# LSH attention with a mixture of experts on one core: in pairs 1 to 13 the products with v of two query blocks run together

## Chip, cores and metric

One core of one Trainium2 chip runs the whole program. The metric is the device time of one execution in microseconds (us). Three executions of the kernel before took 709.75, 714.4 and 717.0 us, median 714.4 us. A further execution was profiled.

## The reference, cut to what matters

The first half is attention over 4 batches, 8 heads, 768 tokens, head size 64. Every query and key gets a code of 6 bits (the signs of six projections), and a query sees only the keys with its own code:

```python
mask = q_bucket[:, :, :, None] == k_bucket[:, :, None, :]
scores = scale * np.matmul(q, k.transpose(0, 1, 3, 2))
scores = np.where(mask, scores, -1000000000.0)
attn = np.exp(scores - np.max(scores, axis=-1, keepdims=True))
attn = attn / (np.sum(attn, axis=-1, keepdims=True) + 1e-09)
return np.matmul(attn, v).astype(np.float32)
```

The second half sends each of the 3072 tokens to the one of 8 experts that a gate picks, and computes `gate * (relu(x @ w1) @ w2)` there. The change touches the attention only.

## The kernel before

**Pairs, groups, steps.** Two heads make a pair: 16 pairs, four of them per batch. The 768 queries of a pair fall into two groups of three query blocks (128 queries each). A step is one block of one head, so a group has 6 steps and a pair 12; the loop over `steps` runs 192 times, and `n` is the step's number in its group. Pairs are counted from 0.

**One step.** `scores` (L227) multiplies a query block with all 768 keys, in four TensorE instructions into one of two PSUM buffers `s` (L232, L233; the second operand adds the low parts and the codes). VectorE reads `s` once, writes `p` and the row maximum (L241), which frees the buffer. ScalarE takes the exponential in place (L250). The result must be transposed before it can meet v. In pairs 1 to 13 the steps n = 0, 2, 4 of a group do this through memory: four DMAs write the block out (L260), one brings it back in another order (L263), and VectorE turns 32x32 squares (L266, the "turn") at the first place of the step six later. The steps n = 1, 3, 5 do it on TensorE (`transposes`, L275) with two copies on ScalarE (L278); these stand in steps n = 2, 4 and n = 0 of the next group.

**The products with v.** `av` (L288) makes 12 matrix products for one query block, 24 instructions of L293, into the single PSUM buffer `o`. A group's products are made while the next group's scores run: before the change its blocks 0, 1 and 2 at n = 1, 3 and 5 of the next group. At n = 5 `av_evac` follows, whose copy of `o` (L300) is made by ScalarE in the next step.

**Order.** The order on TensorE, VectorE, ScalarE and SyncE is that of the program; SyncE issues nearly all DMAs, in order. In loop step i TensorE gets, in this order: the scores of step i + 2; a piece of the tail of an earlier group; the codes of the next pair, if due; transposes; products with v. The scores of step i + 2 need the `s` buffer that VectorE's read of step i frees. VectorE gets: the turn, if one is due; the read of step i + 2; the pieces.

**The tails.** At n = 1 `out_and_route` (L744) handles the group before last. In three of four pairs it is `av_out` (L312): three transposes into the single PSUM buffer `misc` (L323), and a VectorE product that reads it (L324). For the last pair of a batch it is the logits (L344), and `av_out`, `gather_heads` (L356), `one_hot`, a pause, `ranks` (L376 to L386; the last VectorE instruction that reads `misc` is L386) and `rows` follow one per step. So the groups with such pieces are both groups of pairs 4, 8, 12 and the first group of pairs 5, 9, 13.

**The codes.** At n = 3 of a pair's first group `pair_codes` (L141) issues 8 TensorE instructions into `misc` (L146) for the next pair; VectorE reads them (L148). In that step no piece of a tail is issued.

The lines that place the products with v, and the tail's piece of a step:

```python
due.append((i + 2, lambda a=prev[0], c=prev[1]: out_and_route(a, c)))
...
side = (g, n) == (0, 3) and 0 < pr < NPR - 1
if due and due[0][0] == i and not last:
    due.pop(0)[1]()
elif light and not side and (not last or n < 2):
    light.pop(0)()
```

Of the kernel before, what the change touches and what calls it, by code (L numbers as in the profile page):

```python
# [58 lines left out]
def lsh_attention_moe_kernel(ctx, tc, qkd, q2d, k2d, v, pjbd, wg, w1, w2, ident_in, tri_in, cols_in, eoff_in, ids_in, out):  # L59
# [228 lines left out]
    def av(pr, g, jj, o):  # L288
        vt = operands[pr][1]
        pt = probs_t(pr, g, jj)  # L290
        for kc in range(NB):
            for hh in range(2):
                PE.matmul(out=o[hh * D:hh * D + D, jj * P:jj * P + P], lhsT=vt[:, kc, hh * D:hh * D + D], rhs=pt[:, hh, kc],  # L293
                          start=kc == 0, stop=kc == NB - 1)

    def av_evac(pr, g, sums, o, defer):
        b, pi = divmod(pr, NPAIR)
        ot = otp.tile([P, 384], F32, name="ot")
        if defer:
            late.append(lambda: A.copy(out=ot, in_=o[:, 0:384]))  # L300
        else:
            V.tensor_copy(out=ot, in_=o[:, 0:384])
        ots[(b, g, pi)] = ot
        if (b, g) not in invs:
            invs[(b, g)] = smp.tile([P, 3, H], F32, name="inv", bufs=4)
        inv = invs[(b, g)][:, :, 2 * pi:2 * pi + 2]
        if defer:
            divide.append(lambda: V.reciprocal(out=inv, in_=sums.rearrange("p (j h) -> p j h", h=2)))
        else:
            V.reciprocal(out=inv, in_=sums.rearrange("p (j h) -> p j h", h=2))  # L310
# [178 lines left out]
    def early_logits(b, g):  # L489

        inv = invs[(b, g)]
        n = NPAIR - 1
        lsb = gp.tile([P, 384], F32, name="lsb", bufs=1)
        lw = gp.tile([P, 3, H, E], F32, name="lw", bufs=1)
        parts.append(gp.tile([P, 3, E], F32, name="part", bufs=1))

        def logits():
            lps = ps_m.tile([P, 512], F32, name="misc")
            for pi in range(n):
                PE.matmul(out=lps[32 * pi:32 * pi + 32, 0:384], lhsT=wg_sb[:, pi, :], rhs=ots[(b, g, pi)], start=True, stop=True)  # L500
            V.tensor_copy(out=lsb[0:32 * n], in_=lps[0:32 * n, 0:384])

        def gather_heads():
            lt = ps_m.tile([P, 512], F32, name="misc")
            for jj in range(3):
                PE.transpose(out=lt[:, jj * P:jj * P + 32 * n], in_=lsb[0:32 * n, jj * P:jj * P + P], identity=ident[0:32 * n, 0:32 * n])
            for jj in range(3):
                V.tensor_tensor(
                    out=lw[:, jj, 0:2 * n].rearrange("p (q h) e -> p q h e", h=2),
                    in0=lt[:, jj * P:jj * P + 32 * n].rearrange("p (q x) -> p q x", x=32)[:, :, 0:2 * E].rearrange("p q (h e) -> p q h e", h=2),  # L510
                    in1=inv[:, jj, 0:2 * n].rearrange("p (q h) -> p q h", h=2).unsqueeze(3).broadcast_to([P, n, 2, E]),
                    op=ALU.mult)

        def total():
            V.reduce_sum(out=parts[0], in_=lw[:, :, 0:2 * n].rearrange("p j h e -> p j e h"), axis=AX.X)

        return [logits, gather_heads, total]

    NPR = B * NPAIR
    MOVES = {(pr, g): (0, 2, 4) for pr in range(1, NPR - 2) for g in range(2)} | {(14, 0): (0, 2), (14, 1): (0,)}  # L520

    def blocks(pr, g):
        if (pr, g) in MOVES:
            return [(1, 0), (0, 0), (2, 0), (1, 1), (2, 1), (0, 1)], (0, 1, 2)
        b = [(jj, hh) for jj in range(3) for hh in range(2)]
        return sorted(b, key=lambda x: x[::-1]) if (pr, g) == (0, 0) else b, (0, 1, 2)
# [217 lines left out]
    def out_and_route(pr, g):  # L744
        while divide:
            divide.pop(0)()
        if pr % NPAIR < NPAIR - 1:
            av_out(pr, g)
            return

        pieces = route(pr // NPAIR, g)
        pieces[0]()
        light.append(lambda: av_out(pr, g))
        light.extend(pieces[1:])
        if (pr, g) == (NPR - NPAIR - 1, 1):
            light.extend(pick_first(light.pop()))
# [16 lines left out]
    for i, (pr, g, jj, hh) in enumerate(steps):  # L773
        n = i % 6
# [46 lines left out]
        last = pr == NPR - 1 and g == 1  # L821
# [13 lines left out]
        if prev is not None:  # L835
            if n == 0:
                o = ps_o.tile([P, 512], F32, name="o")
            order_p = blocks(prev[0], prev[1])[1]
            for jp in (order_p[:2], order_p[2:])[n] if last and n < 2 else order_p[n // 2:n // 2 + 1] if not last and n % 2 == 1 else ():
                av(prev[0], prev[1], jp, o)  # L840
            if n == (1 if last else 5):
                av_evac(prev[0], prev[1], prev[2], o, (prev[0], prev[1]) != (NPR - 2, 1) and not last)
                if not last:
                    due.append((i + 2, lambda a=prev[0], c=prev[1]: out_and_route(a, c)))
                if (prev[0], prev[1]) == (NPR - 2, 1):
                    light += early_logits(B - 1, 1)
# [240 lines left out]
    with tc.manual_schedule(engines={SY.engine}):  # L1087
# [10 lines left out]
        for e in range(E):  # L1098
            last = e + 1 == E
# [154 lines left out]
```

## Time and profile before

| what | value |
|---|---|
| three executions | 709.75, 714.4, 717.0 us (median 714.4) |
| profiled execution | 719.9 us, of which the span 718.1 us and 1.8 us around it |
| mean granted TensorE clock | 0.992 of full speed |
| TensorE, VectorE, ScalarE, GpSimd busy | 97%, 68%, 61%, 57% of the span |
| pairs 1 to 13 in the trace | from 37.5 to 359.8 us |
| a plain second group of a pair | 11.58 us |
| a plain first group of a pair (with codes) | 12.33 us |
| a group with pieces of a batch's tail | 13.35 to 13.62 us |

Busy time of TensorE is a modelled figure, since its instructions overlap; the starts of its instructions show the pace. A group's time is the distance between the starts of its first scores and of the next group's.

### The profile page before, as it was taken

The page shows a single profiled execution, that of the slowest core. Times are in us where ns is not written, and L with a number is a line of the kernel's source. Part 1 is how long each engine was busy: PE and PEld are TensorE (multiplying, and loading weights), DVE is VectorE, ACT ScalarE, POOL GpSimd, SP SyncE. Part 2 cuts the span into 40 slices and gives each one's busy share as a digit, 9 for nine tenths or more (in the row PEclk, how much of TensorE's full clock was granted, in tenths as well). Part 3 has the DMA queues.
Part 4 walks back from the last instruction along what each step waited for, and adds up shares of the span by engine and source line. Part 5 has one row for each costly group of instructions (what it writes and reads, how often), then busy time and mean ns, then how long its engine had stood idle before and what let it go on. Part 6 is the DMA issues. An engine that isn't in the chain of part 4 may idle for free.

```text
span 718.1 us, 16099 instructions
## 1 busy us (share of the span) xinstructions
PE 696.8 (97%) x5735; PEld 615.9 (86%) x5735; DVE 484.8 (68%) x1012; ACT 439.1 (61%) x996; POOL 408.8 (57%) x410
## 2 busy tenths in 40 slices
PE   7999999999999999999999989999999999999996
PEld 3888887788888888888888869999999999988994
DVE  6667878878778877878787656746464656464641
ACT  6887887788887888877777642434343434334330
POOL 3895757686656866676684320056564654707171
PEclk9999999999999999999999999999999999999999
DMA  8989878989988899799886217474746476665421
GB/s 279 294 258 283 276 232 254 290 261 278 281 260 259 250 291 266 235 289 287 230 251 185 89 62 184 118 196 119 196 135 180 145 208 160 207 163 158 147 70 47
DMA packets 110082, 150.34 MB, mean 209 GB/s; under 512 B 12548, under 2 KB 77990, under 8 KB 109992
## 3 DMA queue, kind: packets, MB, share of 16 engines
q1 hardware_dynamic: 105016, 136.52, 65.6%
q0 software_dynamic: 4976, 12.69, 5.0%
q8 instruction: 47, 0.77, 0.4%
q14 instruction: 43, 0.35, 0.1%
HBM read 94.23 MB, written 55.18 MB: 208 GB/s over the span
## 4 chain that ended last, share of the span: by engine, by line
PE 51%; issue 24%; POOL 13%; DMA 6%; DVE 2%; SPq 1%; ACT 1%; POOLq 0%; another core or an unknown queue 0%; DVEq 0%; ACTq 0%
PE o L293 17%; PE s L232 11%; POOL y L1029 11%; PE s L233 9%; PE t L275 9%; PE misc L146 2%; PE misc L323 2%; POOL yo L1027 2%; DMA y<-yo,tok 2%; DMA xr<-xs 1%; DVE p L241 1%; DMA qk<-qkd 1%; PE s L732 1%; DMA wraw<-w 1%; ACT p L250 1%
## 5 line engine op out<-in xcount | busy, mean ns | idle before, releaser
L232 PE MATMUL s<-k,q 128*128 128x512 f32 (+1 forms) x384 | 149.4, 389 | 0.1
L293 PE MATMUL o<-pt,vt 128*64 128x128 f32 x2304 | 146.8, 277 | 0.0
L293 PEld LDWEIGHTS o<-pt,vt 128*64 128x64 f32 x2304 | 123.8, 137 | 23.5 <-issue 18.4
L241 DVE TENSOR_SCALAR_CACHE_REDUCE p<-s 128x768 f32<-128x768 f32 x111 | 106.0, 955 | 35.9 <-PE s L233 31.6
L278 ACT COPY pt<-t 128x384 f32<-128x384 f32 x222 | 95.7, 482 | 52.6 <-PE t L275 46.0
L233 PE MATMUL s<-c 76*128 76x512 f32 (+1 forms) x384 | 124.1, 344 | 0.0
L1029 POOL DMA_INDIRECT y<-yo,tags x88 | 100.4, 1141 | 24.9 <-issue 22.7
L250 ACT ACTIVATE p<-p,m 128x768 f32<-128x768 f32 x111 | 104.4, 941 | 9.4 <-DVE m L244 6.7
L241 DVE TENSOR_SCALAR_CACHE_REDUCE pd<-s 128x768 f32<-128x768 f32 x81 | 76.8, 948 | 33.1 <-PE s L233 11.0
L232 PEld LDWEIGHTS s<-k,q 128*128 128x128 f32 x384 | 73.3, 191 | 27.6 <-issue 14.8
L987 ACT ACTIVATE hh<-hps 128x352 fp32r<-128x352 f32 (+3 forms) x56 | 27.9, 500 | 105.1 <-PE hps L1001 88.0
L275 PE MATMUL t<-ident,p 128*128 128x128 f32 x666 | 92.0, 274 | 0.1
L266 DVE STREAM_TRANSPOSE pt<-pq 128x768 f32<-128x768 f32 x81 | 78.6, 970 | 14.1 <-DMA pq<-moved 11.7
L701 DVE TENSOR_TENSOR wlo<-wraw,whi 128x1024 fp32r<-128x1024 f32 x60 | 72.9, 1217 | 17.4 <-ACT whi L696 15.7
L233 PEld LDWEIGHTS s<-c 76*128 76x128 f32 x384 | 74.0, 193 | 9.2 <-ACT c L208 0.4
L1020 PE MATMUL hps<-hh,whi 128*128 128x448 f32 (+9 forms) x224 | 77.3, 345 | 2.0 <-ACT whi L696 2.0
L275 PEld LDWEIGHTS t<-ident,p 128*128 128x128 f32 x666 | 75.2, 141 | 4.5 <-issue 2.5
L250 ACT ACTIVATE pd<-pd,m 128x768 f32<-128x768 f32 x81 | 75.9, 937 | 5.2 <-DVE m L244 0.8
L1020 PE MATMUL hps<-hh,wlo 128*128 128x436 f32 (+6 forms) x224 | 77.2, 344 | 1.8 <-DVE wlo L701 1.4
L1027 POOL TENSOR_TENSOR yo<-yt,tags 128x512 f32<-128x512 f32 (+3 forms) x25 | 23.2, 950 | 97.3 <-DVE yt L1022 97.2
L1020 PE MATMUL hps<-hl,whi 128*128 128x436 f32 (+6 forms) x224 | 77.1, 344 | 0.0
L1001 PE MATMUL hps<-xh,whi 128*128 128x352 f32 (+3 forms) x224 | 75.2, 336 | 0.0
(226 smaller groups left out, 1284.0 us busy)
## 6 DMA issues: line engine op xcount, KB each, us to landing
wraw<-w SPq DMA_DIRECT2D x64, 512.0 KB
moved<-pd SPq DMA_DIRECT2D x324, 96.0 KB
pq<-moved SPq DMA_DIRECT2D x81, 384.0 KB
qk<-qkd SPq DMA_DIRECT2D x30, 384.0 KB
xs<-zrow SPq DMA_DIRECT2D x8, 910.0 KB
vt<-v SPq DMA_DIRECT2D x16, 384.0 KB
coded<-cr SPq DMA_DIRECT2D x15, 192.0 KB
c<-coded SPq DMA_DIRECT2D x30, 72.0 KB
```

The costliest lines, as they stand in the source:

```text
L232: PE.matmul(out=s[:, c0:c1], lhsT=q1[:, qs], rhs=k1[:, c0:c1], start=True, stop=False)
L233: PE.matmul(out=s[:, c0:c1], lhsT=q2[0:KM, qs], rhs=k2[0:KM, c0:c1], start=False, stop=True)
L241: V.tensor_scalar(out=to, in0=of, scalar1=-0.5 * BIG, scalar2=None, op0=ALU.max, op1=ALU.max, accum_out=m[:, 0:1])
L250: A.activation(p, p, AF.Exp, bias=m[:, 1:2], scale=0.125, accum_out=sums[:, idx:idx + 1])
L266: V.transpose(out=pt()[:, hh].rearrange("p c (s j) -> p c s j", j=SQ), in_=q.rearrange("p s c i -> p c s i"))
L275: PE.transpose(out=t[:, i * P:i * P + P], in_=p[:, kc * P:kc * P + P], identity=ident)
L278: A.copy(out=dst, in_=src)
L293: PE.matmul(out=o[hh * D:hh * D + D, jj * P:jj * P + P], lhsT=vt[:, kc, hh * D:hh * D + D], rhs=pt[:, hh, kc], start=kc == 0, stop=kc == N ...
L701: loeng.tensor_tensor(out=lo[:, i:i + step], in0=cell["t"], in1=bf(hi[:, i:i + step]), op=ALU.subtract)
L1001: PE.matmul(out=hps[:, 0:w], lhsT=wt[:, c, fs], rhs=xt[:, c, 0:w], start=n == 0, stop=n == 3 * NDC - 1)
L1020: PE.matmul(out=yps[:, 0:w], lhsT=wt[:, f, ds], rhs=ht[:, 0:w], start=n == 0, stop=n == 3 * NFC - 1)
L1029: rows_apart("out", G.indirect_dma_start(out=out_seg, out_offset=bass.IndirectOffsetOnAxis(ap=tags[:, i, 0:1].bitcast(I32), axis=0), in_=y ...
```

## The change

In pairs 1 to 13 (`0 < pr < NPR - 2`, with NPR = 16) nothing is multiplied with v at n = 1 any more; the products of the group's first two blocks are issued together at n = 3, where in a pair's first group they stand behind the codes, and those of the third at n = 5 as before. Pairs 0, 14 and 15 keep their order. No instruction is added or removed on any engine, and no buffer changes.

```diff
-            for jp in (order_p[:2], order_p[2:])[n] if last and n < 2 else order_p[n // 2:n // 2 + 1] if not last and n % 2 == 1 else ():
+            if last:
+                now = (order_p[:2], order_p[2:])[n] if n < 2 else ()
+            elif 0 < pr < NPR - 2:
+                now = {3: order_p[:2], 5: order_p[2:]}.get(n, ())
+            else:
+                now = order_p[n // 2:n // 2 + 1] if n % 2 else ()
+            for jp in now:
                 av(prev[0], prev[1], jp, o)
```

## Rows read from the trace of the kernel before

**Rows 1.** Busy time by stretch (PE, PEld, DVE, ACT, POOL; then clock, DMA share), pair 6, first group

```profile
160.40:172.70 12.30, 12.30 (x128) 10.19 (x126) 9.88 (x19) 9.89 (x26) 8.57 (x9) 1.00 0.97 293
```

**Rows 2.** Timeline of TensorE (start, duration, line), a plain second group, from n = 1

```profile
198.78 0.49 PE L323 MATMUL misc<-ident,ot 128*128 128x128 f32 x3
199.21 1.53 PE L293 MATMUL o<-pt,vt 128*64 128x128 f32 x24
200.67 0.50 PE L232 MATMUL s<-k,q 128*128 128x512 f32 x1
201.01 0.40 PE L233 MATMUL s<-c 76*128 76x512 f32 x1
...
201.49 0.82 PE L275 MATMUL t<-ident,p 128*128 128x128 f32 x6
202.06 0.48 PE L232 MATMUL s<-k,q 128*128 128x512 f32 x1
202.38 0.40 PE L233 MATMUL s<-c 76*128 76x512 f32 x1
```

**Rows 3.** Timeline of TensorE, two cuts of the same products with v

```profile
199.37 1.37 PE L293 MATMUL o<-pt,vt 128*64 128x128 f32 x22
...
200.46 0.28 PE L293 MATMUL o<-pt,vt 128*64 128x128 f32 x2
```

**Rows 4.** Timeline of VectorE, pair 6, first group, n = 0

```profile
161.56 0.98 DVE L266 STREAM_TRANSPOSE pt<-pq 128x768 f32<-128x768 f32 x1 [1.51 <-DMA pq<-moved]
162.46 0.92 DVE L241 TENSOR_SCALAR_CACHE_REDUCE pd<-s 128x768 f32<-128x768 f32 x1
```

**Rows 5.** Timeline of TensorE, the same group, n = 1

```profile
162.54 0.49 PE L323 MATMUL misc<-ident,ot 128*128 128x128 f32 x3
```

**Rows 6.** Timeline of VectorE, pair 11, first group, n = 0

```profile
285.83 0.98 DVE L266 STREAM_TRANSPOSE pt<-pq 128x768 f32<-128x768 f32 x1 [2.24 <-DMA pq<-moved]
```

**Rows 7.** Waits of VectorE by line: total us, times, longest

```profile
DVE pt L266 <- DMA pq<-moved: 11.7, 15, 2.2
```

**Rows 8.** Timeline of VectorE, pair 8, first group, n = 2

```profile
211.96 0.98 DVE L266 STREAM_TRANSPOSE pt<-pq 128x768 f32<-128x768 f32 x1 [0.25 <-DMA pq<-moved]
213.78 0.96 DVE L241 TENSOR_SCALAR_CACHE_REDUCE pd<-s 128x768 f32<-128x768 f32 x1 [0.84 <-DMA pq<-moved]
...
214.66 0.55 DVE L324 TENSOR_TENSOR xr<-misc,inv 128x384 f32<-128x384 f32 x1
```

**Rows 9.** Timeline of TensorE, the codes in pair 8, n = 3

```profile
215.29 0.85 PE L146 MATMUL misc<-qk,pj 128*32 128x384 f32 x8
```

**Rows 10.** Timelines of VectorE and TensorE, pair 4, first group, turn and codes

```profile
112.85 0.98 DVE L266 STREAM_TRANSPOSE pt<-pq 128x768 f32<-128x768 f32 x1 [0.77 <-DMA pq<-moved]
...
115.66 0.85 PE L146 MATMUL misc<-qk,pj 128*32 128x384 f32 x8
```

**Rows 11.** Timelines of VectorE and TensorE, pair 12, first group, turn and codes

```profile
312.76 0.98 DVE L266 STREAM_TRANSPOSE pt<-pq 128x768 f32<-128x768 f32 x1 [0.32 <-DMA pq<-moved]
...
315.12 0.85 PE L146 MATMUL misc<-qk,pj 128*32 128x384 f32 x8
```

**Rows 12.** Timeline of VectorE, pair 4, second group, n = 2

```profile
125.58 0.94 DVE L266 STREAM_TRANSPOSE pt<-pq 128x768 f32<-128x768 f32 x1
127.60 0.96 DVE L241 TENSOR_SCALAR_CACHE_REDUCE pd<-s 128x768 f32<-128x768 f32 x1 [1.08 <-issue]
...
129.06 0.16 DVE L386 TENSOR_SCALAR mx<-misc 128x3 f32<-128x3 f32 x1
```

**Rows 13.** Timeline of TensorE, the same group, n = 3

```profile
129.36 0.52 PE L323 MATMUL misc<-ident,ot 128*128 128x128 f32 x3 [0.18 <-DVE mx L386]
```

**Rows 14.** Busy time by stretch, as in the first group: pair 5, first group, n = 0 to 3

```profile
135.10:142.70 7.60, 7.19 (x69) 5.90 (x65) 7.25 (x22) 6.40 (x20) 6.69 (x6) 1.00 0.90 304
```

**Rows 15.** Timelines of VectorE and TensorE, the same group, n = 2 and 3

```profile
142.54 0.16 DVE L386 TENSOR_SCALAR mx<-misc 128x3 f32<-128x3 f32 x1
...
142.80 0.85 PE L146 MATMUL misc<-qk,pj 128*32 128x384 f32 x8 [0.42 <-PE s L233]
```

## The prediction, made before the kernel was run

> **What bounds the kernel now.** I read the page first, then busy time by stretch, then the timelines of TensorE and VectorE through some groups, and last the waits. In the attention TensorE has no pause at all in a plain group: 12.30 of 12.30 us, against 9.88 on VectorE and 9.89 on ScalarE, with the 16 DMA engines at a share of 0.97 [rows 1]. So TensorE's own order sets the pace, and DMA is the next limit by a few per cent. The reader is to see two more things. Wherever TensorE changes from one kind of work to another it loses some tenths of a microsecond [rows 2, 3]. And VectorE's "turn" of a moved block waits for its DMA 15 times, 11.7 us in all [rows 7], which costs TensorE nothing today: by the time it needs the buffer that VectorE frees behind the turn, VectorE has caught up. The products with v of block 0, at n = 1, are part of that cushion.
>
> **What the change removes and adds on TensorE.** In a plain group the stretch from the three transposes of the tail (198.78) to the second score instruction behind the products with v (201.01) lasts 2.23 us [rows 2]. Without those products the scores follow the transposes directly. No row shows that border with three transposes, but L275 makes the same kind of transpose: from the first of six to the second score instruction it is 202.38 - 201.49 = 0.89 us. Three fewer, at 0.11 each, leave 0.56. Removed: 2.23 - 0.56 = 1.67 us. At n = 3 twelve products join a run that exists already. Their price inside a run: (1.37 - 0.28) / 10 = 0.109 us for two instructions [rows 3], since the cuts differ by 20; twelve make 1.31 us. Saved per group: 1.67 - 1.31 = 0.36 us. If the unseen border cost as much as that of the transposes before the products, 0.43, and the first score then 0.34, the stretch would be 0.77 instead of 0.56 and the saving 0.15. I take 0.36, since L323 and L275 do the same thing.
>
> The Trainium skill speaks against this saving: in "TensorE: Matmul & The Clock Gate", section "Step-by-step: what each phase is for", weight loads are pulled ahead of running products, so a border between two kinds of work would be nearly free and joining two runs worth nothing. The trace does not bear that out: the last product with v starts 0.21 us before the scores (200.46 to 200.67), and inside the run it is 0.109 [rows 2, 3].
>
> Seventeen of the 26 changed groups are plain: 17 x 0.36 = 6.1 us saved. The other nine carry pieces of a batch's tail and are worked out below. No DMA moves in its queue: SyncE issues nothing in the moved step, and POOL neither. The `o` buffer is written later, so the wait for its copy can only shrink; block 0's transposed tile is held two steps longer, and is still read before the next tile needs its place. Both count as nothing.
>
> **What is late next: the `s` buffer at n = 2.** TensorE now reaches the scores of n = 2 directly behind the three transposes, 0.24 us after their start (0.57 for six [rows 2], less 0.33). In pair 6 that is 162.54 + 0.24 = 162.78 [rows 5]. VectorE's read of the buffer starts behind a turn that waited 1.51 us for its DMA, and ends at 162.46 + 0.92 = 163.38 [rows 4]. With 0.08 us for the signal (214.66 + 0.55 = 215.21 to 215.29 [rows 8, 9]) TensorE waits 0.7 us. So a turn may wait up to about 0.8 us there and costs nothing; beyond that every tenth counts. Of the plain first groups three have longer waits, pairs 6, 10 and 11; the longest is 2.24 us in pair 11 [rows 6], so 1.4 us lost there, and for the one between them I take 0.9. Together 3.0 us back. If DMAs land as much earlier as the groups get shorter, less; if they land at the same moments, 0.36 more for each.
>
> **What is late next: `misc` in the tails.** Three kinds of group, three of each. In all of them TensorE waits for a VectorE instruction that reads `misc`, and block 0's products used to run before that wait and now run behind it, for 1.31 us.
> - First groups of pairs 4, 8, 12: the codes wait for L324. Behind its turn VectorE can now go on at once, because the scores are there: turn to read 0.90 us (162.46 - 161.56 [rows 4]), read to L324 0.88, L324 itself 0.55 [rows 8], signal 0.08, together 2.41 us. Pair 8: 211.96 + 2.41 = 214.37 instead of 215.29 [rows 9], 0.92 earlier, so 1.31 - 0.92 = 0.4 us lost. Pair 4: 115.26 instead of 115.66 [rows 10], 0.9 lost. Pair 12: 315.17 instead of 315.12 [rows 11], 1.4 lost. Together 2.7.
> - Second groups of the same pairs: L323 at n = 3 waits for L386. The read could start at 125.58 + 0.90 = 126.48 instead of 127.60, where VectorE stood idle for 1.08 us [rows 12]; so L323 can come 1.1 us earlier than 129.36 [rows 13], and 0.2 us is lost, 0.6 in three.
> - First groups of pairs 5, 9, 13: the codes wait for L386, and VectorE has been at work 7.25 of the 7.60 us before its end at 142.70 [rows 14, 15]. Nothing that TensorE does sooner makes this chain shorter, so the codes stay at 142.80 and the whole 1.31 is lost, 3.9 in three. From the other side: if all 0.35 us of idle time in the chain went, 0.96 each.
>
> **The sum.** - 6.1 + 3.0 + 2.7 + 0.6 + 3.9 = + 4.1 us. The profiled execution, 718.1 us of span and 1.8 around it, would become 724.0. It lies 5.5 us above the median of the three runs (0.8%), so against the median the forecast is 714.4 + 4.1 = 718.5 us. Its own range: with half of the waits of pairs 6, 10, 11 and of the first kind of tail gone, + 1; with 0.36 more in each first group whose turn is late, and one late turn more, + 8: 715 to 722.
>
> **The rivals.**
> **A, the saving comes whole.** DMAs land earlier in step with the groups, VectorE's chain shifts, and no wait appears. For it: the turns' waits come and go from pair to pair, so they hang on moments. Price: 20 x 0.36 in groups with the transposes, 6 x 0.15 in those with logits, 8.1 us: 706.3 us. Against it: the chain in pair 5 has hardly a gap [rows 14].
> **B, DMA becomes the bound, clearly slower.** Place: the turn at the start of a pair's first group. At a share of 0.97 [rows 1] the moved blocks cannot land sooner, so every group that gets 0.36 us shorter makes the next turn that much later, until TensorE waits in all plain first groups. Then the 6.1 us saved are all given back: + 4.1 + 6.1 = + 10.2, 724.6 us. It decides from the point where six of the seven plain first groups have a turn that waits over 0.8 us. Against it: three do now, and plain second groups hardly wait.
> **C, joining runs saves nothing,** as the rule on weight loads would have it: the same + 10.2 us, 724.6 us, with all waits as in the forecast but no 0.36. Against it: rows 2 and 3.
> **D, the order on TensorE stays as it was,** 714.4 us. Against it: the order is the program's.
>
> **Chances.** Forecast 0.55, A 0.19, B 0.18, C 0.05, D 0.03. The range reaches from A to B and C: 706 to 725 us; what is left out is the outer side of these and the scatter of the runs, which is 7 us in three. About 1% (7.1 us) is what a measurement of this kernel can tell from no change. A passes it barely, so faster by over 1% gets 0.15; B, C and the upper end of the forecast give slower by over 1% 0.29; within 1% is 0.56.
>
> **What would show it.** Right: plain second groups shorten from 11.58 to about 11.22 us and L293 stands in runs of 48; first groups of pairs 5, 9, 13 grow by over 1 us; TensorE's waits list several microseconds on the codes (L146) and on the first score instruction (L232). A: no such waits, and all groups shorter. B: turns wait far more than 11.7 us in all. C: 11.58 stays. The forecast is wrong if the groups with tails grow by less than 0.5 us each, or if plain first groups lose more than they gain.

## The result, and the profile after

The change makes the kernel slower: 724.5 us (median of ten runs, 718.4 to 731.4) against 713.7 us for the kernel before beside it (ten runs, 709.8 to 717.0). The ratio is 1.0138, 95% interval 1.0101 to 1.0174, or + 9.8 us. It is that of the means, without one of the ten executions (731.4 us), which lies over 1.5% above the fastest and counts as slow. A second measurement of the same kernel, told below, gave 1.0130 (1.0086 to 1.0175). The forecast of + 4.1 us had the sign and some 40% of the size. Its own range, 715 to 722 us, was missed; the time lies in the wider range of 706 to 725 only because that reached out to rivals B and C at 724.6. To "slower by over 1%" I had given 0.29.

The profiled execution took 726.8 us, its span 725.0. All of the loss lies in pairs 1 to 13. The two spans differ by 6.9 us only, since outside these pairs the profiled execution of before took 395.8 us and this one 389.3; that part of the program was not changed. I measure a group from its first score instruction behind the products with v of the group before to the same instruction of the next group; the 26 groups of pairs 1 to 13 take 335.7 us together against 322.3 before, and 333.1 in the second profile of the changed kernel. By the kinds of group that the forecast told apart, in us against the kernel before:

| groups | forecast | after | after, second profile |
|---|---|---|---|
| ten plain second groups | - 3.6 | - 1.3 | - 2.7 |
| seven plain first groups | + 0.5 | + 7.5 | + 0.5 |
| first groups of 4, 8, 12 | + 2.7 | - 0.3 | + 0.3 |
| second groups of 4, 8, 12 | + 0.6 | + 0.4 | + 0.4 |
| first groups of 5, 9, 13 | + 3.9 | + 7.1 | + 12.3 |
| sum | + 4.1 | + 13.4 | + 10.8 |

**The joined run itself** is what the forecast said. TensorE's timeline of a plain second group (start, duration, engine, line, operation, tiles, shapes, count), which answers to [rows 2]. PE is TensorE, PEld its weight loads, DVE VectorE, ACT ScalarE, POOL GpSimd; in brackets, where they come, stand the engine's idle time before the instruction and what ended it:

```profile
181.85 0.49 PE L323 MATMUL misc<-ident,ot 128*128 128x128 f32 x3
182.10 0.47 PE L232 MATMUL s<-k,q 128*128 128x512 f32 x1
...
184.34 2.84 PE L293 MATMUL o<-pt,vt 128*64 128x128 f32 x48
187.11 0.51 PE L232 MATMUL s<-k,q 128*128 128x512 f32 x1
```

The scores stand directly behind the three transposes, 0.25 us after their start, and 48 products with v form one run. This group is 11.20 us long, the same group before 11.57: 0.37 us saved where 0.36 was forecast. Five of the ten plain second groups came to 11.19 to 11.21 us in this profile and seven in the second one; those right behind the first groups of pairs 5, 9 and 13 gained 0.24 at most.

**TensorE's waits** in the whole of the changed kernel (total us, times, longest):

```profile
PE s L232 <- DVE pd L241: 6.6, 7, 2.0
PE misc L323 <- ACT ot L300: 2.0, 4, 0.6
PE misc L376 <- DVE xr L324: 2.0, 3, 0.7
PE misc L376 <- ACT lsb L348: 1.1, 3, 0.4
PE misc L146 <- PE s L233: 1.0, 2, 0.5
```

In the kernel before no wait of L232 on VectorE is listed, and L376 waits 0.3 us in all. VectorE's turn, which answers to [rows 7]:

```profile
DVE pt L266 <- DMA pq<-moved: 24.2, 15, 3.1
```

As often as before, but twice as long. What a late turn does now is to be seen in pair 6, first group. VectorE's timeline, then TensorE's, answering to [rows 4, 5]:

```profile
166.62 0.98 DVE L266 STREAM_TRANSPOSE pt<-pq 128x768 f32<-128x768 f32 x1 [3.07 <-DMA pq<-moved]
167.52 0.92 DVE L241 TENSOR_SCALAR_CACHE_REDUCE pd<-s 128x768 f32<-128x768 f32 x1
```

```profile
166.04 0.49 PE L323 MATMUL misc<-ident,ot 128*128 128x128 f32 x3
168.51 0.69 PE L232 MATMUL s<-k,q 128*128 128x512 f32 x1 [1.98 <-DVE pd L241]
...
169.85 1.48 PE L275 MATMUL t<-ident,p 128*128 128x128 f32 x6
```

The turn waits 3.07 us, the read of the scores stands behind it, and TensorE has nothing to do for 1.98 us. That is the forecast's mechanism. What the forecast did not have is the last line: six transposes take 1.48 us instead of 0.82. Busy time by stretch (PE, PEld, DVE, ACT, POOL, then granted clock, DMA share, GB/s) shows why:

```profile
166.00:168.50 2.50, 0.53 (x5) 0.29 (x3) 1.88 (x4) 0.07 (x2) 0.87 (x2) 1.00 0.96 310
168.50:170.00 1.50, 1.49 (x5) 1.30 (x6) 1.40 (x4) 1.44 (x5) 1.50 (x1) 0.55 0.94 333
170.00:172.00 2.00, 2.00 (x10) 1.81 (x9) 1.93 (x4) 1.75 (x4) 1.09 (x2) 0.50 0.90 245
172.00:174.00 2.00, 2.00 (x27) 1.23 (x27) 1.44 (x4) 1.64 (x5) 0.00 (x0) 0.98 0.98 259
```

TensorE is busy for 0.53 of 2.50 us, and then the granted clock is 0.50, its lower level of 1.2 GHz, while TensorE has work all the time. The profile of the kernel before shows no such stretch in pairs 1 to 13. The changed kernel has three in this profile (pairs 6, 9 and 10), each behind waits of TensorE of about 2 us: 1.98 in pair 6, 1.85 in pair 10, and 0.27 + 0.62 + 0.39 + 0.65 in pair 9.

**The groups beside the tails.** Pair 5, first group, TensorE's timeline, answering to [rows 15]:

```profile
140.00 0.55 PE L323 MATMUL misc<-ident,ot 128*128 128x128 f32 x3 [0.38 <-ACT ot L300]
140.93 0.50 PE L232 MATMUL s<-k,q 128*128 128x512 f32 x1 [0.39 <-DVE pd L241]
...
142.57 0.40 PE L376 MATMUL misc<-run,ident 128*128 128x24 f32 x2 [0.66 <-DVE xr L324]
...
142.96 0.85 PE L275 MATMUL t<-ident,p 128*128 128x128 f32 x6
...
145.01 0.85 PE L146 MATMUL misc<-qk,pj 128*32 128x384 f32 x8 [0.50 <-PE s L233]
145.79 2.84 PE L293 MATMUL o<-pt,vt 128*64 128x128 f32 x48
```

Where TensorE waited once before the codes, 0.42 us [rows 15], it now waits in four places within some five microseconds, 1.93 us in all. One of them, at L323, is for ScalarE's copy of `o` (L300). In pair 8 the first group went the other way; VectorE and TensorE, answering to [rows 8, 9]:

```profile
219.18 0.56 DVE L324 TENSOR_TENSOR xr<-misc,inv 128x384 f32<-128x384 f32 x1
```

```profile
219.79 0.85 PE L146 MATMUL misc<-qk,pj 128*32 128x384 f32 x8
```

The group's first score starts at 214.02, so the codes come 5.77 us into the group; before it was 215.29 - 208.16 = 7.13. They moved up by 1.36 us, more than the 1.31 us of products taken away, and nothing is lost.

### The profile page after: what moved, and what is told of

It is laid out like the page before. It is cut to its first block, busy times and chain, and to the rows that moved or that the text cites. A ratio compares the mean times of both kernels' runs of the same rounds, so it can differ in the third digit from the quotient of the medians.

```text
span 725.0 us, 16086 instructions
## 1 busy us (share of the span) xinstructions
PE 696.3 (96%) x5735; PEld 618.2 (85%) x5735; DVE 482.2 (67%) x1012; ACT 436.3 (60%) x996; POOL 418.7 (58%) x410
## 4 chain that ended last, share of the span: by engine, by line
issue 20%; POOL 15%; PE 10%; DMA 4%; SPq 1%; DVE 1%; POOLq 0%; another core or an unknown queue 0%; ACT 0%; ACTq 0%; DVEq 0%
POOL y L1035 12%; PE o L293 3%; PE t L275 2%; POOL yo L1033 2%; PE s L232 2%; DMA y<-yo,tok 2%; PE s L233 1%; DMA xr<-xs 1%; PE s L732 1%; DMA wraw<-w 1%; SPq L657 0%; POOL tags L956 0%; DMA xs<-xr,slot 0%; POOL tags L952 0%
## 5 line engine op out<-in xcount | busy, mean ns | idle before, releaser
L232 PE MATMUL s<-k,q 128*128 128x512 f32 (+1 forms) x384 | 150.0, 391 | 7.3 <-DVE pd L241 6.6
L293 PE MATMUL o<-pt,vt 128*64 128x128 f32 x2304 | 142.1, 276 | 0.2 <-DVE pt L266 0.2
L1035 POOL DMA_INDIRECT y<-yo,tags x88 | 106.7, 1213 | 24.9 <-issue 22.6
L232 PEld LDWEIGHTS s<-k,q 128*128 128x128 f32 x384 | 74.2, 193 | 36.6 <-issue 13.7
L275 PE MATMUL t<-ident,p 128*128 128x128 f32 x666 | 94.3, 278 | 0.2
L701 DVE TENSOR_TENSOR wlo<-wraw,whi 128x1024 fp32r<-128x1024 f32 x60 | 74.4, 1241 | 16.7 <-ACT whi L696 16.1
L1026 PE MATMUL hps<-hh,whi 128*128 128x448 f32 (+9 forms) x224 | 75.7, 338 | 0.0
L1026 PE MATMUL hps<-hl,whi 128*128 128x436 f32 (+6 forms) x224 | 75.6, 338 | 0.0
L1026 PE MATMUL hps<-hh,wlo 128*128 128x436 f32 (+6 forms) x224 | 75.6, 338 | 0.0
L1007 PE MATMUL hps<-xl,whi 128*128 128x428 f32 (+6 forms) x224 | 74.8, 334 | 0.0
```

The costliest lines, as they stand in the source:

```text
L232: PE.matmul(out=s[:, c0:c1], lhsT=q1[:, qs], rhs=k1[:, c0:c1], start=True, stop=False)
L275: PE.transpose(out=t[:, i * P:i * P + P], in_=p[:, kc * P:kc * P + P], identity=ident)
L701: loeng.tensor_tensor(out=lo[:, i:i + step], in0=cell["t"], in1=bf(hi[:, i:i + step]), op=ALU.subtract)
L1007: PE.matmul(out=hps[:, 0:w], lhsT=wt[:, c, fs], rhs=xt[:, c, 0:w], start=n == 0, stop=n == 3 * NDC - 1)
L1026: PE.matmul(out=yps[:, 0:w], lhsT=wt[:, f, ds], rhs=ht[:, 0:w], start=n == 0, stop=n == 3 * NFC - 1)
L1035: rows_apart("out", G.indirect_dma_start(out=out_seg, out_offset=bass.IndirectOffsetOnAxis(ap=tags[:, i, 0:1].bitcast(I32), axis=0), in_=y ...
```

## The experiments

All ratios are to the kernel before, run beside each on the same chip. They come from three sets, in which the kernel before had medians of 708.2 us (the parts alone, and the turn behind the read in all steps), 715.3 (the turn at n = 0, less DMA, the first version of two places) and 713.9 (the others). Theory W, as first put: the loss comes from VectorE's read of the scores behind a late turn; each expectation says what W claims there, and names the rival. Changes in us are read from one profiled execution each. The table has the changes by kind of group, in us, against the profile of before (columns as the rows of the table above: plain second, plain first, first of 4/8/12, second of 4/8/12, first of 5/9/13):

| kernel | 2nd | 1st | 4/8/12, 1st | 4/8/12, 2nd | 5/9/13, 1st | sum | ratio |
|---|---|---|---|---|---|---|---|
| second groups alone | - 3.8 | + 0.1 | + 1.6 | 0.0 | - 0.3 | - 2.4 | 0.9957 |
| 17 plain groups | - 2.0 | + 6.1 | - 0.2 | 0.0 | - 1.7 | + 2.2 | 1.0000 |
| nine tail groups | 0.0 | 0.0 | + 0.5 | + 0.4 | + 3.5 | + 4.3 | 1.0062 |
| turn behind read, all steps | + 5.1 | + 2.7 | + 3.0 | + 3.2 | + 5.3 | + 19.2 | 1.0273 |
| turn behind read, n = 0 | - 1.8 | - 1.1 | + 2.2 | + 0.9 | + 8.5 | + 8.6 | 1.0165 |
| two places | - 2.2 | - 0.1 | - 0.1 | + 1.1 | - 2.2 | - 3.5 | 0.9936 |
| not 5/9/13 | - 2.6 | + 5.1 | - 0.3 | + 0.4 | + 2.3 | + 4.9 | 1.0053 |
| not plain first | - 0.7 | + 0.5 | + 3.7 | + 0.4 | + 8.8 | + 12.7 | 1.0136 |
| two places, not 4/8/12 | - 2.8 | - 1.0 | - 0.2 | 0.0 | - 1.2 | - 5.2 | 0.9933 |

### The parts of the change, each alone

The ten plain second groups alone:

```
-            elif 0 < pr < NPR - 2:
+            elif 0 < pr < NPR - 2 and g and pr % NPAIR:
```

> Only the ten plain second groups of pairs 1 to 13 have their products with v of blocks 0 and 1 in one run; all first groups and the groups with pieces of a tail keep the order before. Theory W (TensorE's own border is saved, and what it costs is that TensorE now stands waiting where VectorE is late): each of the ten groups 0.37 us shorter in the trace, no new wait of TensorE, -3.7 us against the kernel before, ratio 0.995. Rival D (DMA is the bound, any gain of pace is given back): the ten groups are shorter but the first groups behind them longer by as much; 0 +- 1 us.

Measured: 0.9957 (0.9938 to 0.9976). Each of the ten is 0.35 to 0.39 us shorter, and the time is what W expected. "No new wait" did not hold: the first groups of pairs 12 and 13, whose order is as before, were 1.6 and 0.8 us longer, with waits at L232, L323 and L146.

The 17 plain groups:

```
-            elif 0 < pr < NPR - 2:
+            elif 0 < pr < NPR - 2 and not TAIL:
```

with TAIL true for the groups of pairs 4, 8, 12 and the first groups of 5, 9, 13.

> All 17 plain groups have the run of two blocks, the nine groups with pieces of a tail keep the order before. In the trace of the changed kernel the 17 gained 0.37 where nothing was late and sum to +6.2 us, because of first groups with a late turn (pairs 3, 6, 10), two of them with a fall of the clock. Theory W with the lateness belonging to the first groups themselves: +3 to +7 us against before. Rival T (the lateness in pairs 6 and 10 was made by the changed tail groups just before them): those two lose nothing and the sum is -3 to -6 us.

Measured: 1.0000 (0.9980 to 1.0021), between the two expectations. The first groups of pairs 6 and 10 lose 0.9 and 1.2 us without the tails joined, so rival T fails. The second groups gain, and the first groups lose 6.1 us to one line of the waits:

```profile
PE s L232 <- DVE pd L241: 6.5, 6, 1.4
```

No stretch of its pairs is at a clock of 0.50. The nine tail groups alone:

```
-            elif 0 < pr < NPR - 2:
+            elif 0 < pr < NPR - 2 and TAIL:
```

> Only the nine groups with pieces of a tail have the run of two blocks. Theory W: no change in pairs 4, 8, 12 (-0.2 to +0.2 us each group), first groups of pairs 5, 9, 13 longer by 1.3 us or more each, with a wait of TensorE on the misc buffer (ranks, codes) and on the score buffer; +4 to +7 us in all. Rival D: as the pace hardly rises, 0 to +2 us.

Measured: 1.0062 (1.0034 to 1.0090), a time within W's expectation; but the first groups of 5 and 9 grew by 0.55 us each instead of 1.3. The plain groups cost nothing in sum and the tails about 0.6%, and together they cost 1.4%: by these ratios the parts don't add up. They were measured in the set at 708.2 us, the whole change beside 713.7 and 713.9; that the other set has no part in it is not shown. With the tails alone one stretch at 0.50 is left, in pair 13 (+ 2.4 us); with both parts there are three.

### VectorE's order

The change with the turn behind the read of the scores in every step:

```
-        while turns and turns[0][0] == i:
-            turns.pop(0)[1]()
...
         if i + 1 < len(steps):
             run_expo(i + 1)
+        while turns and turns[0][0] == i:
+            turns.pop(0)[1]()
```

> The changed kernel, and VectorE's turn stands behind the read of the scores in its step instead of ahead of it, in all groups. Theory W: TensorE no longer waits on the score buffer at n = 2 when a turn is late; waits on L232 fall from 6.6 us to under 2, the falls of the clock in pairs 6, 9, 10 go, and of the +10.9 us at most +4 are left (the waits on misc in pairs 5, 9, 13). Rival D: moving the turn does not bring data sooner, the time stays +8 to +11 us.

Measured: 1.0273 (1.0238 to 1.0309), far above what W and its rival expected. The waits on L232 and the falls of the clock in pairs 1 to 13 are gone, as W expected; in their place:

```profile
PE o L293 <- DVE pt L266: 4.8, 16, 0.4
PE misc L376 <- DVE xr L324: 4.1, 3, 1.4
```

The products at n = 5 now wait for turned rows. To leave those out, the next kernel moved the turn at n = 0 alone (`... == i and n:` at the first place, the second place as above).

> The change, with VectorE's turn of the rows (line 266) put behind the read of the scores (line 241) at the first of a group's six steps (n = 0) alone; in the other five the turn stays ahead of it. In the changed kernel the first turn of a group waits up to 3.07 us for its rows, the read of the scores stands behind it on VectorE, and TensorE waits 1.98 us for the scores' buffer at n = 2 (pair 6). Theory W (the loss comes from that queueing of the read behind a late turn, and from the granted clock of 0.50 that follows the stall): the waits on line 232 fall from 6.6 us to under 2, no stretch of pairs 1 to 13 is left at a clock of 0.50, the first groups of pairs 6, 9 and 10 fall from +3.3 to +3.5 us to under +1, and what is left of the change is the gain of 0.37 us in ten second groups (-3.7) and the waits for misc in the first groups of pairs 5, 9 and 13 (some 1.5 us each): -2 to +3 us, a ratio of 0.997 to 1.004. Rival D (the late rows delay TensorE by other roads too, at the products with v that use the turned rows): the wait moves to the products with v at n = 3 and the ratio stays at 1.010 to 1.015.

Measured: 1.0165 (1.0126 to 1.0204). Half of W held: the plain first groups are 1.1 us shorter than before, and L232 waits 0.3 us on VectorE's reads in all of pairs 1 to 13. But the first groups of 5, 9 and 13 cost 8.5 us, with a stretch at a clock of 0.50 in pairs 5 and 9, and with these waits:

```profile
PE misc L376 <- DVE xr L324: 4.1, 3, 1.4
...
PE misc L146 <- DVE xr L324: 2.7, 3, 1.6
```

So, in this profile, the late turn accounts for the loss of the plain first groups, and is not what most of the loss hangs on.

### Less DMA

All pairs use the v of pair 0, with the change and without it:

```
-            operands[pr + 1][1] = load_v(pr + 1)
+            operands[pr + 1][1] = operands[0][1]
```

> The change, without the loads of v for pairs 1 to 15: all pairs use the v of pair 0, so the output is not that of the reference, and a pair has one transfer less. This and the next kernel differ only by the change. Theory W with the transfers as the cause of the late rows: VectorE's first turn waits under 1 us for its rows in the plain first groups, line 232 shows no wait of a microsecond, no stretch of pairs 1 to 13 is at a clock of 0.50, and the change has a ratio of 0.990 to 1.000 to the next kernel. Rival L (the rows are late by their own way from the store to the read, whatever else is moved): the waits of the turns stay at 20 us or more and the ratio to the next kernel stays at 1.008 to 1.018.

> The kernel before, without the loads of v for pairs 1 to 15 (all pairs use the v of pair 0, so the output is not that of the reference): the counterpart of the kernel ahead of it, without the change. Both theories: the turns' waits fall from 11.7 us to a few, and since TensorE waited little for them the time changes by less than 1 per cent (ratio 0.993 to 1.000).

Measured: 842.5 us with the change and 833.0 without, 1.1778 (1.1714 to 1.1842) and 1.1637 (1.1593 to 1.1680); the one is 1.0114 times the other, as rival L expected. The other values send the tokens to other experts, and the mixture behind the pairs takes over 100 us longer, which I had not expected, so only the pairs can be read. Over 40 to 360 us, first the kernel with the change, then the one without:

```profile
40.00:360.00 320.00, 309.39 (x3129) 261.18 (x3128) 240.24 (x530) 247.79 (x640) 211.26 (x205) 0.98 0.82 241
```

```profile
40.00:360.00 320.00, 318.33 (x3245) 266.65 (x3246) 253.14 (x551) 260.58 (x664) 219.01 (x218) 1.00 0.86 251
```

In these pairs the turns wait 9.5 and 7.4 us in all, and the change still costs 12.0 us in pairs 1 to 13, 12.1 of them in the first groups of 5, 9 and 13, where 5 and 9 have a stretch at a clock of 0.50. Neither expectation held whole: fewer transfers don't save the change, and the loss does not need long waits of the turns.

### The change once more

> The changed kernel once more, for a second profile. Theory W: TensorE stalls of 1.5 us or more come again in the first groups of 6, 9 and 10 or of others that follow a tail, at least two of them followed by a stretch at a clock of 0.50; ratio 1.010 to 1.018. Rival: where the stalls and falls come is chance; then other groups have them, with waits on the scores' buffer of another sum (under 3 us or over 10).

Measured: 1.0130 (1.0086 to 1.0175). VectorE's turns waited only 7.5 us in these pairs, and the loss was the same. The rival was right about the places, though not about L232, which waited 3.2 us: pair 6 lost 0.4 us this time instead of 3.5, and the stretches at 0.50 stand in pairs 5, 9 and 13. Pair 5, TensorE's timeline and then busy time by stretch:

```profile
137.04 0.55 PE L323 MATMUL misc<-ident,ot 128*128 128x128 f32 x3 [0.62 <-ACT ot L300]
137.98 0.52 PE L232 MATMUL s<-k,q 128*128 128x512 f32 x1 [0.39 <-DVE pd L241]
...
139.62 0.62 PE L376 MATMUL misc<-run,ident 128*128 128x24 f32 x2 [0.26 <-DVE xr L324]
...
140.24 1.52 PE L275 MATMUL t<-ident,p 128*128 128x128 f32 x6
...
142.97 1.51 PE L146 MATMUL misc<-qk,pj 128*32 128x384 f32 x8
```

```profile
136.00:138.00 2.00, 0.99 (x7) 0.53 (x5) 2.00 (x6) 1.79 (x6) 1.92 (x2) 1.00 1.04 354
138.00:140.00 2.00, 1.74 (x6) 1.30 (x7) 1.90 (x5) 1.94 (x6) 1.31 (x2) 0.58 0.68 228
140.00:142.00 2.00, 2.00 (x16) 1.90 (x16) 1.82 (x7) 1.27 (x5) 0.00 (x0) 0.50 0.81 202
142.00:144.00 2.00, 2.00 (x12) 0.85 (x10) 0.92 (x2) 1.41 (x4) 0.00 (x0) 0.50 0.68 202
```

VectorE has no gap from 136 to 138; TensorE stands idle for half of that time, in front of L323 and L232. Then the clock is 0.50 through codes and transposes, and the group is 4.2 us longer than before. In the first profile, without such a stretch, the same group was 1.6 us longer, with waits of 1.93 us against 1.50 here. So the low clock cost some 3 us here, if nothing else sets the two apart.

The low clock is not all of the loss. Of the six executions of this measurement two had a mean clock of 0.995 and 0.996, within the 0.992 to 0.999 of the kernel before beside it, and took 722.2 and 723.4 us all the same.

### Without the first groups of 5, 9 and 13, and without the plain first groups

```
-            elif 0 < pr < NPR - 2:
+            elif 0 < pr < NPR - 2 and (g or pr not in (5, 9, 13)):
```

> The change, undone in three groups alone: the first groups of pairs 5, 9 and 13 keep the order before. In the profile of the changed kernel these three grow by 7.1 us together, and the first groups of pairs 6 and 10, which come two groups later, by 6.8 us. Theory W (the lateness starts beside the tails and is handed on through VectorE and the moved blocks): the first groups of 6 and 10 fall back to at most +1.3 us, as in the kernel where no tail group is joined, no stretch of pairs 1 to 13 is at a clock of 0.50, and the time is that of the kernel with the 17 plain groups: a ratio of 0.998 to 1.004. Rival D (each group pays for itself): pairs 6 and 10 stay at +3 us with their falls of the clock, and the ratio is 1.004 to 1.009.

Measured: 1.0053 (1.0022 to 1.0085), some 0.8% below the whole change. The point lies in rival D's range, and the interval reaches into W's. The profile has something of both: pairs 6 and 10 fall back to + 1.8 and + 0.8 us, and no stretch at 0.50 is left in pairs 1 to 13, though L232 still waits 5.7 us on VectorE. This is one execution, of 714.1 us where the median is 718.2. Whole pairs 1 to 13, first the kernel before, then the change (first and second profile), then this kernel:

```profile
37.48:359.76 322.28, 320.17 (x3257) 267.89 (x3255) 253.81 (x549) 261.03 (x665) 220.56 (x217) 1.00 0.89 266
```

```profile
37.39:373.08 335.69, 322.42 (x3256) 272.39 (x3254) 250.26 (x553) 258.44 (x667) 221.02 (x219) 0.98 0.85 256
```

```profile
37.34:370.45 333.11, 323.50 (x3257) 273.36 (x3255) 251.37 (x553) 258.96 (x667) 220.62 (x219) 0.97 0.86 257
```

```profile
36.94:364.09 327.15, 316.53 (x3257) 268.20 (x3255) 249.55 (x549) 257.67 (x665) 220.38 (x217) 1.00 0.88 264
```

TensorE is idle for 2.1, 13.3, 9.6 and 10.6 us, and busy for 320.2, 322.4, 323.5 and 316.5. The idle time of the last two is the same within a microsecond. What sets them apart is the busy time: the same products take 7.0 us longer at a mean clock of 0.97, though three groups more are joined. In all three profiles with joined runs the idle time has grown by 7.5 to 11.2 us. So the loss has two parts, the idle time and the slower work behind some of it.

The other side, the change without the seven plain first groups:

```
-            elif 0 < pr < NPR - 2:
+            elif 0 < pr < NPR - 2 and (g or pr in (4, 5, 8, 9, 12, 13)):
```

> The change, undone in the seven plain first groups (pairs 1, 2, 3, 6, 7, 10 and 11): joined are the ten plain second groups (-3.1 us by themselves) and the nine groups beside the tails (+4.4 us by themselves). If parts add up: +1.3 us, a ratio of 0.999 to 1.005, with the first groups of 5, 9 and 13 at +0.5 to +2.4 us as in the kernel with the tails alone, and the plain first groups at 0. Theory W (a tail's group costs more when the groups ahead of it run faster, since the moved blocks then land later against it): 5 and 9 grow by 1.5 us or more each, with a fall of the clock, and the ratio is 1.004 to 1.010.

Measured: 1.0136 (1.0087 to 1.0185), the whole loss. The parts as measured alone don't add up to it; W's direction holds, its size was too small. 5 and 9 grow by 2.4 and 2.3 us without a fall of the clock, 13 by 4.1 with one. The first groups of 4 and 12 grow by 2.6 and 1.2 us, with the codes waiting 1.05 and 1.13 us for L324. Pair 13:

```profile
347.00:349.00 2.00, 1.49 (x5) 0.98 (x4) 1.91 (x7) 1.73 (x7) 1.58 (x2) 0.66 0.73 214
349.00:351.00 2.00, 1.96 (x15) 1.96 (x16) 1.90 (x6) 1.44 (x4) 0.00 (x0) 0.50 0.64 148
```

The plain first groups need not be joined for the loss; the joined second groups with the joined groups beside the tails are enough.

### Another order of the same joining

If the missing work at n = 1 is the cause, first groups should keep block 0 there and join blocks 1 and 2 at n = 5:

```
-                now = {3: order_p[:2], 5: order_p[2:]}.get(n, ())
+                now = {3: order_p[:2], 5: order_p[2:]}.get(n, ()) if g and pr % NPAIR else {1: order_p[:1], 5: order_p[1:]}.get(n, ())
```

> Another order of the same joining: in the plain second groups of pairs 1 to 13 blocks 0 and 1 run together at n = 3, as in the change; in all first groups and in the groups beside the mixture's tails block 0 stays at n = 1, where it was, and blocks 1 and 2 run together at n = 5. So every group has one run less, and none has its first work with v later than n = 1. Theory W (a joined run is worth 0.37 us; the loss comes from what the missing work at n = 1 lets run too early against the late turns and the tails' work): every group of pairs 1 to 13 is 0.2 to 0.4 us shorter, no wait of a microsecond on line 232, clock 1.0 throughout the pairs: -5 to -9.6 us, a ratio of 0.987 to 0.993. Rival D (block 1 at n = 5 only moves the wait: its work is missing at n = 3): first groups and tails as long as before and a ratio of 0.994 to 1.000, no better than the kernel with the ten second groups alone (0.9957).

Measured: 0.9936 (0.9905 to 0.9967), between W's range and the rival's. Right in direction, but the gain is 3.5 us in the pairs and not 5 to 9.6: five of seven plain first groups gain some 0.15 us each, and the second groups of 4, 8, 12 lose 0.3 to 0.4. So these and the first groups of 4, 8, 12 were put back:

```
-            elif 0 < pr < NPR - 2:
+            elif 0 < pr < NPR - 2 and g and pr % NPAIR:
                 now = {3: order_p[:2], 5: order_p[2:]}.get(n, ())
+            elif 0 < pr < NPR - 2 and not g and pr % NPAIR:
+                now = {1: order_p[:1], 5: order_p[1:]}.get(n, ())
```

> The order with two places (plain second groups: blocks 0 and 1 at n = 3; first groups: block 0 at n = 1, blocks 1 and 2 together at n = 5), without the six groups of pairs 4, 8 and 12, which keep the order before. In the kernel that had it in them too, their second groups were 0.3 to 0.4 us longer and their first groups as long as before. So 1 us less than that kernel, if parts add up: a ratio of 0.990 to 0.995, second groups of 4, 8 and 12 at 13.35 us. Rival: the gain of 0.7 us in the first groups of 5, 9 and 13 hung on the joined groups ahead of them and falls to 0.2: 0.994 to 0.998.

Measured: 0.9933 (0.9905 to 0.9960), 708.1 us beside 713.9; the second groups of 4, 8, 12 are back at their length before. The rival's premise came true in two of three groups: the first groups of 9 and 13 gain 0.25 us now, that of 5 still 0.7. Pair 5, first group, in its profile:

```profile
135.71 0.49 PE L323 MATMUL misc<-ident,ot 128*128 128x128 f32 x3
136.13 1.53 PE L293 MATMUL o<-pt,vt 128*64 128x128 f32 x24
137.59 0.50 PE L232 MATMUL s<-k,q 128*128 128x512 f32 x1
...
140.41 0.85 PE L146 MATMUL misc<-qk,pj 128*32 128x384 f32 x8 [0.15 <-PE s L233]
...
143.47 2.84 PE L293 MATMUL o<-pt,vt 128*64 128x128 f32 x48
```

The 24 products stand between L323 and the scores again, and of the four waits of this group one is left, 0.15 us; in pairs 9 and 13 it is 0.40, as before the change. This is the fastest order tried; from the first version of it and from the second groups alone (0.9957) the intervals don't part it.

## Why the prediction was right in sign and short in size

- **The saving** of 0.36 us per joined run was right: 0.35 to 0.39 measured in the ten second groups alone. No row showed the border behind three transposes; it came to 0.25 us (181.85 to 182.10) where 0.24 was worked out. Rival C, that joining saves nothing, is refuted.
- **The score buffer behind late turns** (+ 3.0 us in pairs 6, 10, 11) was right as a mechanism: the turn that waits, the read behind it, L232; taking the turn out of the way removed the wait. Which pairs it strikes was read off one execution as if it were fixed. In the profiles of the change the plain first groups came to + 7.5 and + 0.5 us. That the second equals the forecast's sum is luck: pair 10 lost 1.4 us there, and pair 11, to which the longest wait was given, gained 0.2.
- **First groups of 4, 8, 12** (+ 2.7 us) did not come: - 0.3 and + 0.3. I let the chain of VectorE start behind a turn at its old time [rows 8]. In pair 8 the turn itself came 0.35 us earlier in the group, and the codes 1.36 us earlier, not 0.92. The wait that it named is real, though: without the plain first groups joined, the codes of pairs 4 and 12 waited for L324, and those groups lost 2.6 and 1.2 us.
- **Second groups of 4, 8, 12** (+ 0.6 us) came to + 0.4: right.
- **First groups of 5, 9, 13** (+ 3.9 us) is the term that was mis-sized: + 7.1 and + 12.3. The place was right, and so was the reason that VectorE's chain there has no slack to come sooner [rows 14]. The wait was put only at the codes, though; it comes at L323, L232, L376 and L146, the first of them for ScalarE, which the forecast named as the cause of no wait, and behind it the clock can fall. I had costed waits as time lost once, with the work after them at full speed. In the second profile TensorE's busy time in pairs 1 to 13 is 7.0 us above that of the kernel without these three groups, where no stretch is at half clock; the whole loss there is 10.8. In the first profile there are three shorter stretches. The rows of pair 6 give 0.9 x 1.5 + 2.0 + 0.04 x 2.0 = 3.4 us at 0.50 (the clock of each row taken as a mean of 1.00 and 0.50). Half of it is lost where TensorE has work throughout, so some 5 us for three, as an estimate.
- **Rival B** named nearly the right time for a wrong reason, and C the same time by chance. B needed six of seven plain first groups late; the loss is whole without joining any of them.
- By the marks set beforehand: 11.20 us, runs of 48, waits on L232 and the growth of 5, 9 and 13 came as named. Waits on L146 stayed at 1.0 us; they stand at L376 and L323 instead. Two marks of a wrong forecast came true as well: six of nine tail groups grew by less than 0.5 us, and in the first profile plain first groups lost more than they gained.

Open: why the tails cost 3.5 us in the first groups of 5, 9 and 13 when joined alone and 8.8 when the plain second groups ahead of them are joined too. In pair 5 the waits at L376 and L146 are there both times (0.66 and 0.50 us alone, 0.67 and 0.49 then); those at L323 for ScalarE (0.63) and at L232 behind it (0.39) are new. Whether the joined groups ahead bring them, or the other set of runs, is not shown. Open too: what makes the waits of one execution fall in pairs 6 and 10 and those of another in 5 and 13. The price of the clock was read from rows at both levels; no kernel kept TensorE busy through the wait to measure it by itself.

## What to carry to other kernels

Before work is taken out of a place in an in-order engine's queue, list the steps around that place which wait on another engine, and ask whether that engine's chain can come sooner: where it can (pair 8) the work was no cover and moving it was free, where it has no gap (pair 5) the work was the cover. Join runs at places with no such step beside them: the gain is then kept, 0.37 us in most plain second groups, 0.15 in the first groups joined at n = 5. And cost a wait of some microseconds on TensorE by what stands behind it as well, since the work after it may run at half clock.

## What the runs showed of the hardware

A short idle time of TensorE could cost more than itself. In pair 6 it was busy for 0.53 of 2.50 us and in pair 5 of the second profile for 0.99 of 2.00; both times the granted clock then went from 1.00 to 0.50 and stayed there for microseconds in which TensorE was busy without a gap. At the lower level six transposes took 1.48 to 1.52 us instead of 0.82 to 0.85, and the eight products of the codes 1.51 instead of 0.85. The sum of the waits alone does not tell where it happens: in the first profile pairs 5 and 9 had 1.93 us each in their first groups, and pair 9 lost its clock while pair 5 kept it. Nor does one long wait: in the kernel without the first groups of 5, 9 and 13 joined, TensorE waited 1.89 us in pair 6, was busy for 0.45 of 2.00 us, and the clock stayed at 1.00.

```profile
164.00:166.00 2.00, 0.45 (x2) 0.41 (x3) 2.00 (x4) 0.44 (x2) 1.36 (x2) 1.00 0.88 278
166.00:168.00 2.00, 2.00 (x18) 1.71 (x20) 1.71 (x5) 1.97 (x6) 1.96 (x2) 1.00 0.97 331
```
